# Feature transposes and their copy moved ahead of the numerators and of a weight piece's rounding, in the attention steps of an attention and two-layer kernel

## The chip, the cores and the metric

The kernel runs on one core of one Trainium2 chip. The metric is the device time of a whole execution in microseconds. Several executions are timed, and their median is the figure that counts. One more execution is recorded by the hardware profiler, and all rows below are from that one.

## The reference

Attention with random features, then two dense layers, all in float32:

```
phi(x) = exp(h - max(h)) / sqrt(m),  h = x @ omega.T - sum(x*x)/2
kv  = einsum('bhsm,bhsd->bhmd', phi(k), v);   z = sum_s phi(k)
num = einsum('bhsm,bhmd->bhsd', phi(q), kv);  den = phi(q) . z + 1e-6
x   = (num / den), heads side by side: 2304 tokens x 512
h = x @ w_in;  g = max(h,0) + alpha*min(h,0);  x = g @ w_out      (512 -> 2048 -> 512)
out = ((x @ w_a) * (x @ w_b)) @ w_out2                            (512 -> 1536 -> 512)
```

There are 4 batches, 8 heads, 576 positions, a head dimension of 64 and 128 features.

## The kernel before, in words

**Attention.** The 32 heads are handled as 8 units of four heads, and each unit as 5 tiles of up to 128 positions (the fifth has 64). One attention step `s` works on several tiles at once, as a software pipeline written out by hand. It projects the keys of tile `s` and the queries of another tile onto the features (`a_proj`, matmuls into the PSUM tiles `pp`), takes their negated maxima on VectorE (`a_max`, `nm`), and takes the exponentials on ScalarE (`a_exp`, `ph`). Then `attn_2` does four things. `a_kv` adds the key features of the step before into `kv`. `a_t` transposes on TensorE the query features that were made two steps before (PSUM tile `tp`) and copies them to SBUF (`phT`, line 798 where the copy is on ScalarE). `a_num` multiplies the transposed features that the step before left by `kv` into the PSUM tile `nd` and divides: three operations on VectorE, `rc`, its reciprocal, and `xn`. The fourth thing is the weight decoder, below. Last, `attn_3` calls `a_x`, which transposes the `xn` of the step before (PSUM tile `xp`) and copies it into the layer's input `xT` (line 839 where the copy is on ScalarE). The PSUM tiles `pp`, `tp`, `nd`, `xp` and the layer's `h` share five banks that go round. So the features are transposed two steps after their projection, their numerators follow one step later, and the transposes of the result one step after that.

**The decoder.** The weights come as 8-byte floats, and a weight piece of 128x512 is turned into two float32 halves, a rounded high one and a low one, whose products make up a precise matmul. `D_.go(n)` advances a Python generator `n` times, and each advance writes out a few instructions. For a piece in this stage (`piece`, line 283) the first three advances are the bits: four VectorE operations, on `z`, `a`, `c` and `c` again; in the first advance GpSimd is also given the scaling `z` of the next piece. The fourth advance is the rounding: `w<-a` on ScalarE (line 290), then a subtraction and an addition, `a<-a,w` and `w<-a,c` (lines 294 and 295), on GpSimd or on VectorE. In `attn_2` the call `D_.go(3)` writes out the bits ahead of everything else, and the call `D_.go()` behind the numerators writes out the rounding. Up to step 14 a piece is begun in about every second step, and from step 15 in each, until 17 pieces fill the places that there are.

**The order of the work.** Each engine takes its instructions in the order in which the program writes them. Until step 14 the attention steps stand alone. From step 15 a step is written inside a step of the first layer (`Mlp.step`): twelve matmuls of 256 columns (`h`), then the step's projections, key products, numerators and transposes, then twelve matmuls of the layer's second half (`y`), then `a_x`. The layer adds for each step `u` and `gh` on ScalarE and `h` and `gl` on VectorE.

**The planner's tallies.** Where an operation can go to two engines, `pick` (line 138) takes the way after which the largest of three tallies, `load["dve"]`, `load["act"]` and `load["pool"]`, is smallest; between equals it takes the first way. Every call books its estimated cost as it is written out, and `passed` takes an allowance of microseconds off all three at each step, 4.5 in steps 6 to 14. The feature copy books 0.62 on ScalarE or 0.70 on VectorE, the numerators of four slots book 0.87 on VectorE, and the copy of the transposed result books 0.41 on ScalarE or 0.37 on VectorE. Which engine gets a piece's subtraction and addition is settled in its first advance.

Of the kernel before, what the change touches and what calls it, by code (L numbers as in the profile page):

```python
# [65 lines left out]
def tile_kernel(ctx: ExitStack, tc: tile.TileContext, qT, kT, v1, omT, wbits, alpha, out):  # L66
# [71 lines left out]
    def pick(*ways):  # L138

        def worst(w):  # L140
            return max(load[e] + w.get(e, 0.0) for e in load)

        i = min(range(len(ways)), key=lambda i: worst(ways[i]))
        for e, x in ways[i].items():
            load[e] += x
        return i
# [579 lines left out]
    def slots_of(t):  # L726
        return 4 if t < 4 else 2

    def bank(name, pool=None):
        return (pool or psp[0]).tile([P, 512], F32, tag="ps", name=name)  # L730
# [39 lines left out]
    def a_kv(u, t):  # L770
        if t == 0:
            kvt[u] = pskv.tile([P, 4, D + 1], F32, tag="kv", name=f"kv{u}")
        kv = kvt[u]
        ph = phik.pop((u, t))
        for h in range(4):

            for r in (slice(0, M // 2), slice(M // 2, M)):
                tensor.matmul(kv[r, h, :], lhsT=ph[:, h if t < 4 else h % 2, r],
                                 rhs=t_v[u][:, t * VC + h * (D + 1):t * VC + (h + 1) * (D + 1)],
                                 start=(t == 0 and h == 0), stop=(t == 4 and h == 3))  # L780
        if t == 4:

            load["act"] += 0.4
            nc.scalar.activation(kvp[u % 3], kv, AF.Copy)
            kvt.pop(u)

    def a_t(u, t):

        ns = slots_of(t)
        ph = phiq.pop((u, t))  # L790
        pp = bank(f"tp{u}_{t}").rearrange("p (o m) -> p o m", m=P)
        for h in range(ns):
            tensor.transpose(pp[:, h, :], ph[:, h, :], ident)
        d = pq.tile([P, 4, P], F32, tag="phT", name=f"phT{u}_{t}", bufs=2)
        if pick({"act": 0.1 + 0.13 * ns}, {"dve": 0.1 + 0.15 * ns}):
            vector.tensor_copy(d[:, :ns], pp[:, :ns])
        else:
            nc.scalar.activation(d[:, :ns], pp[:, :ns], AF.Copy)
        phT[u, t] = d

    def a_num(u, t):


        ns = slots_of(t)
        d = phT.pop((u, t))
        kv = kvp[u % 3]
        nd = bank(f"nd{u}_{t}")[:, :4 * (D + 1)].rearrange("p (o e) -> p o e", e=D + 1)
        for h in range(ns):
            for a in range(2):
                r = slice(a * 64, a * 64 + 64)  # L810

                tensor.matmul(nd[r, h, :], lhsT=d[:, h, r], rhs=kv[:, h if t < 4 else 2 * a + h, :],
                                 start=True, stop=True)
        load["dve"] += 0.35 + 0.13 * ns
        rc = sm.tile([P, 4], F32, tag="rc", name=f"rc{u}_{t}")
        vector.tensor_scalar(out=rc[:, :ns], in0=nd[:, :ns, D], scalar1=EPS * M, scalar2=None, op0=ALU.add)
        vector.reciprocal(out=rc[:, :ns], in_=rc[:, :ns])
        xn = pq.tile([P, 4, D], F32, tag="xn", name=f"xn{u}_{t}", bufs=2)
        vector.tensor_tensor(out=xn[:, :ns], in0=nd[:, :ns, 0:D],
                                in1=rc[:, :ns].unsqueeze(2).to_broadcast([P, ns, D]), op=ALU.mult)  # L820
        xns[u, t] = xn
# [20 lines left out]
    ev = {n: {} for n in ("k", "kv", "q", "t", "num", "x")}  # L842
# [6 lines left out]
    for b in range(NB):  # L849
        u = HG * b  # L850
        for i, ut in enumerate([(u, 0), (u, 1), (u + 1, 0), (u + 1, 1), (u, 2), (u, 3), (u, 4),
                                (u + 1, 2), (u + 1, 3), (u + 1, 4)]):
            s = HG * TT * b + Q_LAG + i
# [37 lines left out]
    def attn_2(s):  # L891

        D_.go(3)
        if s in late:
            held[late[s]] = ev["kv"][s]
        elif s in ev["kv"]:
            for ut in (held.pop(s, None), ev["kv"][s]):
                if ut:
                    a_kv(*ut)
        if s in ev["num"]:  # L900
            a_num(*ev["num"][s])
        D_.go()
        if s in ev["t"]:
            a_t(*ev["t"][s])

    def attn_3(s):
        if s in ev["x"]:
# [20 lines left out]
    if True:  # L928
        w_ = bank("warm")
        for i in range(WARM):  # L930
            tensor.matmul(w_[:, 0:P], lhsT=warm, rhs=warm, start=True, stop=True)
        for s in range(SPLIT_AT):
            D_.step(DEC0[0] if s < 3 else DEC0[1] if s < Q_LAG else DEC0[2])
            passed(1.3 if s < Q_LAG else 4.5)
            pj = attn_1(s)
            nm = a_max(*pj)
            loads(s)

            for k in range(KT):
                if s > x_step[k // 2, (CI - 1) // P]:  # L940
                    A.split(0, 0, CI, k)
            a_exp(*pj, nm)
            if s == 3:
                D_.start(0)
            if s == Q_LAG + 1:
                nc.sync.dma_start(out=bend, in_=alpha)
            attn_2(s)
            attn_3(s)
        vector.tensor_scalar(out=bend, in0=bend, scalar1=-1.0, scalar2=1.0, op0=ALU.mult, op1=ALU.add)
    st_z.close()  # L950

    with st_m:
# [4 lines left out]
        def attn_next(high=None, low=None):  # L957
            s = nxt_s[0]
            nxt_s[0] += 1
            D_.step(DEC1)  # L960
            pj = attn_1(s)
            if high:
                high()
            if pj:
                nm = a_max(*pj)
            loads(s)
            if low:
                low()
            if pj:
                a_exp(*pj, nm)  # L970
            attn_2(s)
            A.after.append(lambda: attn_3(s))
# [381 lines left out]
```

## Time and profile before

| what | us |
|---|---|
| median of the runs (3) | 956.07 |
| lowest and highest | 954.65, 956.70 |
| the profiled execution, its own time | 954.51 |
| span of the profiled execution | 952.7 |
| busy: TensorE, VectorE, ScalarE, GpSimd | 937.4, 677.1, 483.3, 130.6 |

The span runs from the first to the last instruction of the profiled execution; its own time is 1.8 us longer. Matmuls are pipelined and their ends are modelled, so a busy TensorE isn't one at its peak. In the rows PE is TensorE, PEld its weight loads, DVE VectorE, ACT ScalarE, POOL GpSimd. A row of the order in time has the start, the duration, the engine and line, the operation, the written tile and what it reads, and in brackets the idle time before it with what ended it. Most TensorE and VectorE instructions go through a helper and show its line, L188, so tiles tell them apart. The granted TensorE clock is at full speed (1.00) in every stretch.

### The profile page before, as it was taken

To read this page: it belongs to the slowest core of one execution; us is meant where nothing else is said; L and a number is where in the kernel's file an instruction comes from. 1 tells how busy PE (TensorE), PEld (TensorE's weight loads), DVE (VectorE), ACT (ScalarE), POOL (GpSimd) and SP (SyncE) were. 2 spreads that over 40 slices of the span, in tenths; PEclk is the share of its full clock that TensorE was granted. 3 is DMA by queue.
4 is the path that set the end of the run, shared out by engine and by line. 5 is a ranking of instruction groups with operands and counts; after the bars stand their busy time and mean duration, and the time that the engine had idled before them with its cause. 6 is when DMAs were issued, how large, how long until landed. Compare 5 with 4: busy or idle time off the path is not lost.

```text
span 952.7 us, 16709 instructions
## 1 busy us (share of the span) xinstructions
PE 937.4 (98%) x6486; PEld 845.7 (89%) x6486; DVE 677.1 (71%) x1359; ACT 483.3 (51%) x1149; POOL 130.6 (14%) x110
## 2 busy tenths in 40 slices
PE   8889999999999999999999999999999999999998
PEld 7778999999988888889888899999999998989896
DVE  5898854554488888788787977888397867473633
ACT  5876766654344445244444455564364654454541
POOL 3686700000001111010010000000011111110201
PEclk9999999999999999999999999999999999999999
DMA  8544422000133232325538656259829379624323
GB/s 301 172 164 146 140 77 77 26 23 24 46 88 111 89 130 92 133 70 196 184 126 298 254 210 221 78 177 360 305 85 264 94 215 331 181 34 100 47 53 67
DMA packets 49279, 137.88 MB, mean 145 GB/s; under 512 B 4528, under 2 KB 11056, under 8 KB 49200
## 3 DMA queue, kind: packets, MB, share of 16 engines
q1 hardware_dynamic: 44304, 128.03, 38.6%
q0 software_dynamic: 4752, 8.65, 6.0%
q8 instruction: 51, 0.84, 0.4%
q14 instruction: 28, 0.23, 0.1%
q10 hardware_dynamic: 144, 0.13, 0.0%
HBM read 90.14 MB, written 46.66 MB: 144 GB/s over the span
## 4 chain that ended last, share of the span: by engine, by line
PE 91%; DVE 5%; ACT 3%; issue 1%; ACTq 0%; DVEq 0%
PE y L188 21%; PE h L188 20%; PE W L188 16%; PE o L188 15%; PE E L188 8%; PE B L188 4%; ACT ph L765 2%; PE tp L188 1%; PE nd L188 1%; PE kv L188 1%; PE xp L188 1%; DVE c L188 1%; DVE a L188 0%; DVE xl L505 0%; DVE h L188 0%
## 5 line engine op out<-in xcount | busy, mean ns | idle before, releaser
L188 PE MATMUL h<-xh,w 128*128 128x256 f32 (+1 forms) x768 | 204.4, 340 | 0.2 <-DVE yo L188 0.2
L188 PE MATMUL y<-gh,w 128*128 128x256 f32 (+1 forms) x768 | 201.9, 338 | 0.3 <-ACT gh L545 0.3
L188 PEld LDWEIGHTS h<-xh,w 128*128 128x128 f32 x768 | 135.0, 189 | 15.7 <-DVE yo L188 0.4
L188 PEld LDWEIGHTS y<-gh,w 128*128 128x128 f32 x768 | 134.5, 189 | 15.5 <-ACT gh L545 0.5
L188 PE MATMUL o<-w,gh 128*128 128x512 f32 x432 | 133.2, 390 | 0.0
L188 PE MATMUL h<-xl,w 128*128 128x512 f32 (+1 forms) x384 | 129.1, 336 | 0.3 <-DVE xl L505 0.3
L188 PE MATMUL y<-gl,w 128*128 128x512 f32 (+1 forms) x384 | 129.1, 336 | 0.1
L188 DVE SCALAR_TENSOR_TENSOR h<-u,bend,h 128x256 f32<-128x256 f32 (+1 forms) x96 | 59.4, 619 | 58.9 <-ACT u L533 58.5
L533 ACT ACTIVATE u<-h 128x256 f32<-128x256 f32 (+1 forms) x96 | 47.1, 491 | 103.9 <-PE h L188 100.6
L188 PEld LDWEIGHTS o<-w,gh 128*128 128x128 f32 x432 | 81.0, 188 | 16.4
L545 ACT ACTIVATE gh<-h 128x256 fp32r<-128x256 f32 (+1 forms) x96 | 47.1, 491 | 86.0 <-DVE h L188 85.9
L188 PE MATMUL o<-w,gl 128*128 128x512 f32 x216 | 84.2, 390 | 0.0
L1253 POOL DMA_DIRECT2D out<-op x30 | 26.3, 875 | 418.1 <-ACT op L163 337.3
L188 PEld LDWEIGHTS h<-xl,w 128*128 128x128 f32 x384 | 72.7, 189 | 7.9 <-DVE xl L505 0.5
L188 PEld LDWEIGHTS y<-gl,w 128*128 128x128 f32 x384 | 72.8, 190 | 7.8 <-DVE gl L188 0.3
L505 POOL TENSOR_TENSOR xl<-xT,xh 128x512 fp32r<-128x512 f32 (+1 forms) x19 | 25.5, 1358 | 342.8 <-ACT xh L501 187.1
L188 DVE TENSOR_TENSOR gl<-h,gh 128x256 fp32r<-128x256 f32 (+1 forms) x96 | 53.1, 554 | 22.0 <-ACT gh L545 21.4
L163 ACT ACTIVATE u<-W 128x384 f32<-128x384 f32 x72 | 35.1, 492 | 45.7 <-PE W L188 44.4
L163 ACT ACTIVATE op<-o 128x512 f32<-128x512 f32 x51 | 30.4, 597 | 50.7 <-PE o L188 44.8
L188 DVE SCALAR_TENSOR_TENSOR a<-raw,z 128x512 uint32<-128x512 uint32 x68 | 51.1, 751 | 2.1
L188 DVE SCALAR_TENSOR_TENSOR c<-raw,c 128x512 f32<-128x512 uint32 x68 | 48.5, 713 | 2.3
L188 PEld LDWEIGHTS o<-w,gl 128*128 128x128 f32 x216 | 40.6, 188 | 8.4
(491 smaller groups left out, 1942.2 us busy)
## 6 DMA issues: line engine op xcount, KB each, us to landing
raw<-in_w SPq DMA_DIRECT2D x68, 512.0 KB, 4.2
w<-store SPq DMA_DIRECT2D x44, 512.0 KB, 6.9
store<-t_None SPq DMA_DIRECT2D x39, 512.0 KB, 3.0
st<-ypart SPq DMA_DIRECT2D x14, 768.0 KB, 7.0
out<-op POOLq DMA_DIRECT2D x30, 256.0 KB, 5.3
q<-in_qT SPq DMA_DIRECT2D x8, 576.0 KB, 3.8
v<-in_v SPq DMA_DIRECT2D x7, 650.0 KB, 5.8
yp<-ypart SPq DMA_DIRECT2D x4, 1024.0 KB, 7.8
```

What stands on the lines that cost most here:

```text
L163: nc.scalar.activation(out, in_, AF.Copy)
L188: return call(*a, **k)
L505: (nc.vector, nc.gpsimd)[way].tensor_tensor(out=lo, in0=src, in1=hi.bitcast(F32), op=ALU.subtract)
L533: nc.scalar.activation(u_, hp, AF.Relu, scale=-1.0)
L545: nc.scalar.activation(gh, hp, AF.Copy)
L765: nc.scalar.activation(ph[:, 2 * pr + j], pair[j][:, o + pr], AF.Exp, bias=nm[:, j, o + pr:o + pr + 1])
L1253: nc.gpsimd.dma_start(out=dst, in_=op, accum_op=ALU.add)
```

## The change

In `attn_2` the call of `a_t` moves from the end to a place ahead of `a_num`. The order was bits, key products, numerators, rounding, transposes with their copy; it becomes bits, key products, transposes with their copy, numerators, rounding.

```diff
@@ -897,11 +897,11 @@
             for ut in (held.pop(s, None), ev["kv"][s]):
                 if ut:
                     a_kv(*ut)
+        if s in ev["t"]:
+            a_t(*ev["t"][s])
         if s in ev["num"]:
             a_num(*ev["num"][s])
         D_.go()
-        if s in ev["t"]:
-            a_t(*ev["t"][s])
 
     def attn_3(s):
         if s in ev["x"]:
```

## Rows read from the trace of the kernel before

The kinds of row are those of the section on time and profile.

**Rows 1.** Busy time by stage: stretch, length, then busy us of each engine

```profile
14.00:45.00 31.00, 26.12 (x432) 21.91 (x429) 27.64 (x63) 26.08 (x88) 19.61 (x14) 1.00 0.70 238
...
45.00:125.00 80.00, 75.99 (x942) 68.45 (x940) 69.60 (x160) 53.88 (x167) 55.91 (x38) 1.00 0.42 137
...
125.00:240.00 115.00, 114.33 (x1371) 106.95 (x1372) 59.52 (x179) 68.31 (x216) 0.00 (x0) 1.00 0.14 45
```

**Rows 2.** Groups by line and shape, 0 to 330 us: copies and rounding

```profile
L798 ACT ACTIVATE phT<-tp 128x512 f32<-128x512 f32 x32 | 20.0, 624 | 0.0
...
L839 ACT ACTIVATE xT<-xp 128x256 f32<-128x256 f32 x26 | 10.3, 398 | 5.2 <-PE xp L188 5.1
...
L188 DVE COPY xT<-xp 128x256 f32<-128x256 f32 x6 | 2.5, 419 | 2.2 <-PE xp L188 2.2
...
L290 ACT ACTIVATE w<-a 128x512 fp32r<-128x512 f32 x28 | 18.1, 645 | 11.7 <-DVE a L188 11.5
```

**Rows 3.** Who waited for whom, TensorE alone, 14 to 125 us

```profile
PE nd L188 <- ACT phT L798: 2.5, 4, 1.2
...
PE pp(4, 1)_False L188 <- ACT phT L798: 0.2, 1, 0.2
```

**Rows 4.** ScalarE in order of time, step 8

```profile
22.29 2.22 ACT L765 ACTIVATE ph<-pp(1, 3)_False,nm(0, 1, 3)_443 128x128 f32<-128x128 f32 x8
...
24.29 0.75 ACT L290 ACTIVATE w<-a 128x512 fp32r<-128x512 f32 x1
...
24.81 0.71 ACT L798 ACTIVATE phT<-tp 128x512 f32<-128x512 f32 x1
```

**Rows 5.** TensorE in order of time, steps 9 and 10

```profile
23.71 0.69 PE L188 MATMUL kv<-v,ph 128*64 128x65 f32 x16
...
25.57 0.69 PE L188 MATMUL nd<-kvp,phT 128*64 128x65 f32 x16 [1.18 <-ACT phT L798]
...
26.19 0.66 PE L188 MATMUL tp<-ident,ph 128*128 128x128 f32 x4
...
26.78 0.71 PE L188 MATMUL pp(2, 0)_False<-xT,k 64*128 64x128 f32 x8
```

**Rows 6.** VectorE in order of time: idle times, 28 to 48 us

```profile
28.04 1.29 DVE L188 TENSOR_REDUCE nm(0, 2, 0)_544<-pp(2, 0)_False 128x4 f32<-128x512 f32 x2 [0.90 <-PE pp(2, 0)_False L188]
...
34.79 1.02 DVE L188 TENSOR_REDUCE nm(0, 2, 2)_671<-pp(2, 2)_False 128x3 f32<-128x384 f32 x2 [0.20 <-PE pp(2, 2)_False L188]
...
43.33 0.76 DVE L505 TENSOR_TENSOR xl<-xT,xh 128x256 fp32r<-128x256 f32 x2 [0.30 <-ACT xh L501]
```

**Rows 7.** Groups by line and shape, 0 to 330 us: VectorE, two widths

```profile
L188 DVE SCALAR_TENSOR_TENSOR h<-u,bend,h 128x256 f32<-128x256 f32 x40 | 19.4, 486 | 34.7 <-ACT u L533 34.5
...
L188 DVE SCALAR_TENSOR_TENSOR h<-u,bend,h 128x512 f32<-128x512 f32 x15 | 11.3, 752 | 5.0 <-ACT u L533 4.9
```

**Rows 8.** Who waited for whom, 14 to 125 us: around the rounding

```profile
POOL a L294 <- ACT w L290: 25.2, 15, 6.0
...
ACT w L290 <- DVE a L188: 1.8, 6, 0.5
```

**Rows 9.** GpSimd, then TensorE, in order of time: piece 6, its reader

```profile
58.41 1.28 POOL L295 TENSOR_TENSOR w<-a,c 128x512 fp32r<-128x512 f32 x1
...
61.30 0.36 PE L188 MATMUL h<-xh,w 128*128 128x256 f32 x1
```

**Rows 10.** VectorE twice, then GpSimd, in order of time: one decode operation

```profile
76.22 0.42 DVE L188 TENSOR_SCALAR z<-z 128x512 uint32<-128x512 uint32 x1
...
81.17 0.76 DVE L188 TENSOR_SCALAR z<-z 128x512 uint32<-128x512 uint32 x1
...
81.00 1.53 POOL L251 TENSOR_SCALAR z<-raw 128x512 f32<-128x512 f32 x1
```

**Rows 11.** TensorE, then VectorE, in order of time: numerators and reader

```profile
80.17 0.64 PE L188 MATMUL nd<-kvp,phT 128*64 128x65 f32 x16
...
83.77 0.15 DVE L188 TENSOR_SCALAR rc<-nd 128x4 f32<-128x4 f32 x1
```

## The prediction

> **What bounds the kernel now.** I read the busy time by stage first. The moved call runs only in the attention steps, which end before 240 us. From 125 to 240 us TensorE is busy 114.33 of 115 us, with VectorE at 59.52 and ScalarE at 68.31 [rows 1]: there TensorE is the bound, and an order inside the step can't give it more than the 0.67 us that it idles. From 14 to 45 us the picture is another one: VectorE is busy 27.64 of 31 us, ScalarE 26.08, TensorE 26.12, and from 45 to 125 us TensorE idles 4.0 us of 80, with VectorE at 69.60 [rows 1]. So only the stretch from 14 to 125 us is open, and what counts in it is VectorE's line of work and what holds TensorE.
>
> The second view is TensorE's waits in that stretch. The numerators wait four times for the feature copy, 2.5 us together, and once a projection waits 0.2 us for it [rows 3]. The third view shows why. At step 8 ScalarE finishes its exponentials, rounds a piece at 24.29 and only then copies the features at 24.81 [rows 4]; TensorE has ended the key products at 24.40 and starts the numerators at 25.57, after 1.18 us idle [rows 5]. The rounding, whose result GpSimd needs and nobody else soon, stands ahead of a copy that TensorE needs in the next step.
>
> The fourth view is VectorE in order of time, since a wait of TensorE is only worth what it passes on. From 28 to 48 us VectorE idles three times: 0.90 us for a projection, 0.20 us for another and 0.30 us for the rounding of the layer's input on ScalarE, 1.40 us together [rows 6]. The rest of that stretch it works without a gap.
>
> **The change part by part.** Nothing is removed or added in the program's text: four transposes and one copy go ahead of 16 matmuls and three VectorE operations, and ahead of the rounding (one ScalarE operation and, for the 17 pieces of this stage, two on GpSimd). The moved call issues no DMA, nor do the numerators and the rounding, so SP's queue is as it was, and GpSimd's queue keeps its own order.
>
> *TensorE.* The transposes' inputs were made two steps earlier, so they can run as soon as the key products end. At step 9 the transposes would fill 0.6 us from 24.40 on [rows 5]. At step 8 the copy would start at 24.29 instead of 24.81, 0.52 us earlier, and with its 0.71 us end at 25.00 [rows 4]. The numerators then start at about 25.0 and end 0.6 us later, at 25.6; the next projection, which before followed the transposes at 26.78 [rows 5], starts at 25.6, over a microsecond earlier. The first idle time of VectorE, 0.90 us, goes. The same swap takes out the other three waits on the copy, and with them most of the 0.20 us.
>
> *Which engine copies.* This is the part that the diff doesn't show. All 40 feature copies are on ScalarE now (the row has the 32 wide ones), and a few result copies are on VectorE [rows 2]. `a_t` now picks before `a_num` has booked its 0.87 on VectorE. Take a step of the first stage in which no piece is begun, such as 11 or 13. The maxima book 8 x 0.17 = 1.36 on VectorE and the exponentials 8 x 0.28 = 2.24 on ScalarE. Before, the copy saw VectorE at 1.36 + 0.87 = 2.23: on ScalarE the largest tally becomes 2.86, on VectorE 2.93, so ScalarE. After, it sees 1.36: on VectorE that is 2.06, below ScalarE's 2.24, so the copy goes to VectorE. The result copy then sees VectorE at 2.93 and ScalarE at 2.24 and goes to ScalarE (largest tally 2.93 against 3.30); before, it saw 2.23 and 2.86 and went to VectorE (2.86 against 3.27). Step 9 flips its feature copy too (1.02 + 0.70 = 1.72 against 1.68 + 0.62 = 2.30) and has no result copy. In steps with a piece VectorE carries 2.3 more and nothing flips. From step 15 on VectorE's tally runs ahead as long as there is a piece in each step, and what flips long after that lies where TensorE is the bound.
>
> So VectorE gets three wide feature copies and loses two result copies of 0.42 us [rows 2]. The trace has no copy of 512 columns from PSUM on VectorE. It can't cost less than the 256-column copy, 0.42 [rows 2], nor should it cost more than a two-input operation of 512 columns, 0.75 [rows 7]. I take 0.68: the 0.42 plus what the two-input operation adds from 256 to 512 columns, 0.752 - 0.486 = 0.266 [rows 7]. Then VectorE's line grows by 3 x 0.68 - 2 x 0.42 = 1.20 us (by the bounds, 0.42 to 1.41).
>
> *The rest of ScalarE.* The rounding now comes behind the copy, about 0.5 us later (the copy's place in rows 4 is 0.5 to 0.7 us). Where ScalarE waited for the decoder's bits before the rounding, 1.8 us in six cases [rows 8], the copy fills the gap and the delay is smaller. The sum of ScalarE's work ahead of the result copy is the same, so the result copy and the layer's input rounding stand where they stood, or come up to 0.5 us earlier. That, with the result copy's move, covers the 0.30 us of the last idle time.
>
> *Who waits for the later rounding.* GpSimd's subtraction does; it waits for it 25.2 us in 15 cases [rows 8], so GpSimd shifts. What waits for GpSimd is the layer's matmul that reads the low half. The nearest case is piece 6: its addition ends at 59.69, and its reader starts at 61.30 [rows 9]. A delay of 0.5 us, and a reader that comes a little earlier, fit in those 1.6 us, so I cost it at nothing; were that cover gone, TensorE would idle for what is beyond it.
>
> *Who waits for the later numerators.* They come one set of transposes, 0.6 us, later on TensorE. Their first reader on VectorE stands behind the bits: in a typical step the numerators start at 80.17 and end by 80.8, and the reader comes at 83.77 [rows 11]. Behind that reader VectorE has the next step's `h` and maxima. With 3 us of cover it costs nothing in steps with a piece. In steps without one the copy, or the maxima, stand in front of it.
>
> **The sum.** VectorE's line loses 1.40 us of idle time and gains 1.20 us of copies: 0.2 us less (by the bounds of the copy, 1.0 less to nothing). From 45 us on the work of a step is the same on each engine and the 0.2 us is handed through. The 0.2 us of the one projection [rows 3] falls in a stretch in which VectorE has no gap, and I count nothing for it. Against the profiled execution's own time that is 954.51 - 0.2 = 954.3 us. The median of the runs stands 1.56 us above that execution, so the forecast is 956.07 - 0.2 = 955.9 us. A measurement of this kernel can tell about 0.2%, 1.9 us, from no change: this is no measurable change.
>
> **The rivals.**
>
> *TensorE's waits come back in full.* If the numerators' 2.5 us and the projection's 0.2 us [rows 3] were the true bound, the time would be 956.07 - 2.7 = 953.4 us. For it: each ends at the copy, and the copy stood behind the rounding. Against it: VectorE has only 1.40 us of idle time to give where these waits lie [rows 6]. Chance 0.13.
>
> *The swap costs and nothing comes back.* The change then does something else than it says: it moves work onto the fullest engine. If the three idle times only shift to another wait (the next one in line is VectorE's maxima behind the copy), the line grows by the 1.20 us: 957.3 us. Chance 0.12.
>
> *Nothing passes.* Gains and copies end inside the waits that TensorE has anyway between 45 and 125 us, 4.0 us in all [rows 1]: 956.1 us. Chance 0.18.
>
> *VectorE meets GpSimd (slower).* The `z` operation of a piece takes 0.42 us alone and took 0.76 us when it began right behind the start of a GpSimd operation of 1.53 us [rows 10]; 7 of the 17 in this stage took 0.6 us or more. A rounding 0.5 us later shifts GpSimd's three operations against VectorE's bits. If the ten undisturbed ones were all caught, VectorE would lose 10 x 0.34 = 3.4 us, and the time would be 955.9 + 3.4 = 959.3 us. It passes the 1.9 us from the seventh on. Against it: seven already are caught, and a shift frees some as it catches others. The Trainium skill, "SBUF — State Buffer", section "SBUF: two separate sides", says that VectorE and GpSimd share a pair of SBUF ports under an exclusive lock, so that the later of the two stops until the other's instruction ends. By that rule the loss in rows 10 would have been the 1.36 us to the end of GpSimd's operation and not 0.34; the trace bears out a collision, but not one of full length. With 1.36 us each, ten more would make 13.6 us and a time of 969.5 us, and two would already decide. Chance 0.06.
>
> **How the numbers follow.** The forecast has the remaining 0.51. Faster by over 0.2% is the first rival alone, 0.13; slower is the last, 0.06; the forecast and the two middle rivals (957.3 and 956.1 us are both within 1.9 us) make 0.81 for no change. The range takes in the forecast with the copy's bounds, 955.1 to 956.1 us, and the swap at 957.3, and leaves out the two outer rivals, 0.19. The runs of before lie from 954.65 to 956.70, so I add 1.2 us below and 0.6 us above: 953.9 to 957.9 us.
>
> **What would show it.** Right: three feature copies on VectorE ahead of 45 us at 0.65 to 0.7 us each, two result copies fewer there; TensorE's wait of the numerators for the copy near zero; the idle 0.90 us of VectorE at 28 us down to about 0.2; the stage from 125 us on begun 0 to 0.5 us earlier. Wrong: numerators that still wait for the copy, a projection or a maximum that waits for a copy on VectorE, layer matmuls that wait for GpSimd's addition, `z` operations of 0.7 us or more in over ten of the 17, or a second stage whose busy time has changed.

## The result, and the profile after

| what | before | after |
|---|---|---|
| median of 5 runs each, us | 955.58 | 960.39 |
| lowest and highest, us | 954.65, 956.70 | 959.66, 962.03 |
| profiled execution, its own time and span, us | 954.51, 952.7 | 960.39, 958.6 |

The ratio is 1.0059, 95% interval [1.0046, 1.0073]: the kernel became slower by 4.8 us, and the whole interval lies above the 0.2% that a measurement can tell. The forecast was no change, 955.9 us in a range up to 957.9.

What the change was to do early, it did. First ScalarE in order of time at step 8, as in [rows 4] (start, duration, engine, line, operation):

```profile
24.16 0.72 ACT L798 ACTIVATE phT<-tp 128x512 f32<-128x512 f32 x1
24.64 0.76 ACT L290 ACTIVATE w<-a 128x512 fp32r<-128x512 f32 x1
```

And TensorE at steps 9 and 10, as in [rows 5]:

```profile
24.20 0.66 PE L188 MATMUL tp<-ident,ph 128*128 128x128 f32 x4
24.93 0.69 PE L188 MATMUL nd<-kvp,phT 128*64 128x65 f32 x16
25.55 0.71 PE L188 MATMUL pp(2, 0)_False<-xT,k 64*128 64x128 f32 x8
```

The copy now precedes the rounding, the numerators start at 24.93 instead of 25.57 with no idle time of 1.18 us ahead of them, and the next projection comes at 25.55 instead of 26.78. TensorE's waits from 14 to 135 us (engine, tile, line, whom it waited for, total us, times, longest) have no row of the numerators for the copy any more:

```profile
PE xp L188 <- ACT ph L765: 2.4, 3, 1.6
PE kv L188 <- ACT ph L765: 2.0, 3, 0.8
...
PE nd L188 <- DVE xn L188: 0.3, 1, 0.3
```

The copies by line and shape, 0 to 330 us, as in [rows 2]:

```profile
L798 ACT ACTIVATE phT<-tp 128x512 f32<-128x512 f32 x27 | 17.3, 641 | 0.0
L839 ACT ACTIVATE xT<-xp 128x256 f32<-128x256 f32 x32 | 13.1, 409 | 10.7 <-PE xp L188 10.6
L188 DVE COPY phT<-tp 128x512 f32<-128x512 f32 x5 | 3.4, 681 | 0.0
```

Five wide feature copies went to VectorE, at 681 ns each, and all result copies to ScalarE. VectorE got 3.4 us of wide feature copies and lost the 2.5 us of result copies of [rows 2], which is too little for 4.8 us. The busy time by stage, as in [rows 1], does not say at first sight where they lie:

```profile
14.00:45.00 31.00, 27.91 (x438) 22.91 (x436) 29.06 (x65) 25.85 (x89) 19.55 (x14) 1.00 0.69 237
45.00:125.00 80.00, 75.48 (x932) 67.17 (x933) 70.21 (x157) 52.62 (x164) 55.00 (x38) 1.00 0.41 135
125.00:240.00 115.00, 114.63 (x1342) 103.86 (x1338) 58.97 (x173) 67.63 (x214) 0.00 (x0) 1.00 0.14 46
```

From 125 to 240 us TensorE is as busy as before, 114.63 us against 114.33, and has done 1342 matmuls where it had done 1371. It idles no more than before and gets less done. To see when, I follow one landmark through both traces: the first matmul `h` of each first-layer group. The 13th and the 36th, before:

```profile
119.16 0.36 PE L188 MATMUL h<-xh,w 128*128 128x256 f32 x1
...
236.90 0.36 PE L188 MATMUL h<-xh,w 128*128 128x256 f32 x1
```

And after:

```profile
119.45 0.36 PE L188 MATMUL h<-xh,w 128*128 128x256 f32 x1
...
241.50 0.36 PE L188 MATMUL h<-xh,w 128*128 128x256 f32 x1
```

| group | 1st | 9th | 13th | 24th | 32nd | 36th |
|---|---|---|---|---|---|---|
| start before, us | 44.07 | 95.14 | 119.16 | 181.31 | 222.06 | 236.90 |
| after less before, us | -1.15 | -0.01 | +0.29 | +2.86 | +4.53 | +4.60 |

The first layer matmul starts 1.15 us earlier, the gain is used up by the ninth group, and from the 13th to the 36th the changed kernel takes 122.05 us where the other took 117.74: 4.31 us more, with hardly any idle time on TensorE. The busy time of that stretch (stretch, length, then TensorE, its weight loads, VectorE, ScalarE, GpSimd, the granted clock, DMA share and GB/s), before and after:

```profile
119.16:236.90 117.74, 116.89 (x1422) 108.96 (x1421) 62.58 (x186) 69.06 (x218) 2.31 (x2) 1.00 0.14 46
119.45:241.50 122.05, 121.68 (x1422) 110.42 (x1421) 63.45 (x183) 69.91 (x220) 2.14 (x2) 1.00 0.14 44
```

The same 1422 matmuls keep TensorE busy for 121.68 us instead of 116.89, at the same clock, and it idles 0.37 us instead of 0.85. Another 1.3 us come between 566 and 572 us of the kernel before, long behind the attention; they are left open below. Together, -1.15 + 1.44 (up to the 13th group) + 4.31 + 1.3 make the 5.9 us that lie between the two profiled executions; the medians lie 4.8 us apart.

One step there, number 1 of unit 7, TensorE in order of time. Before:

```profile
172.64 0.69 PE L188 MATMUL kv<-v,ph 128*64 128x65 f32 x16
173.16 0.64 PE L188 MATMUL nd<-kvp,phT 128*64 128x65 f32 x16
173.73 0.66 PE L188 MATMUL tp<-ident,ph 128*128 128x128 f32 x4
174.14 0.36 PE L188 MATMUL y<-gh,w 128*128 128x256 f32 x1
```

After:

```profile
174.84 0.69 PE L188 MATMUL kv<-v,ph 128*64 128x65 f32 x16
175.45 0.66 PE L188 MATMUL tp<-ident,ph 128*128 128x128 f32 x4
176.04 0.69 PE L188 MATMUL nd<-kvp,phT 128*64 128x65 f32 x16
176.66 0.38 PE L188 MATMUL y<-gh,w 128*128 128x256 f32 x1
```

The same records of matmuls, 16, 16 and 4, take 1.50 us from the first key product to `y` before and 1.82 us after: 0.32 us more for another order. Look at the part of the array that a row names (rows times columns, 128*64 or 128*128). Key products and numerators fill half its columns, transposes and layer matmuls all. The old order changes the shape once behind the key products, the new one three times. From 130 to 232 us, the median time from the start of the last matmul of one kind to the start of the first of the next:

| boundary | before, ns | after, ns |
|---|---|---|
| `kv` to `nd`, same shape | 49 (12 times) | none |
| `nd` to `tp`, change | 150 (19) | none |
| `tp` to `y`, same shape | 28 (14) | none |
| `kv` to `tp`, change | none | 150 (12) |
| `tp` to `nd`, change | none | 202 (18) |
| `nd` to `y`, change | none | 149 (14) |

Since they run from start to start, these times contain the pace of the earlier kind; inside the groups before, the mean is 31 ns between key products, 29 between numerators and 131 between transposes. In a step that has all three boundaries they sum to 0.501 us against 0.227, 0.27 us more; the other 0.05 us of the step are the numerators themselves, 0.62 us to the next start where it was 0.57 with a boundary of the same length behind them. Why they take longer behind transposes is not shown. In that window: 12 x 0.101 + 18 x 0.052 + 14 x 0.121 = 3.84 us. Between the two landmarks, with the boundaries of every kind counted, the boundaries add 3.8 us and the matmuls inside the groups 1.0 us (0.7 of it the numerators), and TensorE idles 0.5 us less: 4.3 us.

### The profile page after: what moved, and what is told of

Its sections match the earlier page's. It is cut to its first block, busy times and chain, and to the rows that moved or that the text cites. A ratio compares the mean times of both kernels' runs of the same rounds, so it can differ in the third digit from the quotient of the medians.

```text
span 958.6 us, 16703 instructions
## 1 busy us (share of the span) xinstructions
PE 944.2 (98%) x6486; PEld 846.7 (88%) x6486; DVE 680.8 (71%) x1358; ACT 483.2 (50%) x1150; POOL 129.7 (14%) x110
## 4 chain that ended last, share of the span: by engine, by line
PE 86%; DVE 9%; ACT 2%; DMA 2%; issue 1%; SPq 0%; ACTq 0%; DVEq 0%
PE h L188 20%; PE y L188 19%; PE o L188 15%; PE W L188 14%; PE E L188 7%; PE B L188 3%; PE nd L188 1%; DVE c L188 1%; DMA store<-t_None 1%; PE tp L188 1%; ACT ph L765 1%; PE kv L188 1%; DVE a L188 1%; PE xp L188 1%; DVE h L188 1%
```

## The experiments

Theory A: TensorE is held up wherever consecutive matmuls change the shape of the array, and the change adds two such places to each step. Theory B: the feature copies that moved to VectorE cost the time. Theory C: the later rounding does, through GpSimd and its collisions with VectorE. Each kernel was timed 5 to 12 times, beside the kernel before on the same chip, whose median stands in brackets. "Step" below is the time from the first key product to `y` in step 1 of unit 7 (in the first experiment from the first transpose, which there stands in front; the eighth has no such stretch), "loss" the lag behind the kernel before that is added between the 13th and the 36th group; both are from one profile of each kernel.

| experiment | order in the step | median, us (before) | ratio, interval | step, us | loss, us |
|---|---|---|---|---|---|
| (before) | kv, nd, rounding, tp | | 1 | 1.50 | 0 |
| (after) | kv, tp, nd, rounding | 960.39 (955.58) | 1.0059 [1.0046, 1.0073] | 1.82 | 4.31 |
| e1_transposes_first | tp, kv, nd, rounding | 957.87 (955.05) | 1.0032 [1.0020, 1.0044] | 1.67 | 2.82 |
| e2_numerators_first | kv, nd, tp, rounding | 953.68 (955.05) | 0.9993 [0.9984, 1.0003] | 1.50 | 0.02 |
| e3_half_transposes | as after, tp in halves | 962.31 (955.05) | 1.0084 [1.0070, 1.0097] | 1.96 | 7.24 |
| e4_copies_scalar | as after | 960.50 (955.05) | 1.0061 [1.0049, 1.0074] | 1.82 | 4.29 |
| e5_rounding_early | kv, rounding, tp, nd | 961.75 (954.22) | 1.0073 [1.0061, 1.0085] | 1.81 | 4.28 |
| e6_split_transposes | kv, half nd, half tp, half nd, half tp, with the rounding behind nd | 961.19 (954.22) | 1.0067 [1.0054, 1.0080] | 1.80 | 5.04 |
| e7_wide_numerators | as after, nd on all columns | 962.98 (954.22) | 1.0080 [1.0068, 1.0093] | 1.92 | 5.51 |
| e8_transposes_at_layer | tp ahead of the projections | 955.95 (954.44) | 1.0017 [1.0008, 1.0026] | | 1.50 |
| e9_numerators_first_again | kv, nd, tp, rounding | 953.55 (954.44) | 0.9991 [0.9982, 1.0001] | 1.49 | 0.02 |

**One change of shape more instead of two.** In `attn_2`, against the kernel after, the transposes go ahead of the key products:

```diff
         D_.go(3)
+        if s in ev["t"]:
+            a_t(*ev["t"][s])
         if s in late:
...
-        if s in ev["t"]:
-            a_t(*ev["t"][s])
         if s in ev["num"]:
```

> Theory A (array shape): a change between matmuls that fill half of the array's columns (key products, numerators) and those that fill all of them (transposes, layers) holds TensorE up by 0.15 to 0.2 us, and the changed kernel has two such changes more in each step. With the transposes ahead of the key products there is one more than in the kernel before, so from 130 to 230 us a step should lose about 0.17 us against before, half of the changed kernel's 0.33: 957.5 us (956.5 to 958.5). Theory B (the copies that went to VectorE) and theory C (the later rounding and GpSimd's collisions) have the same copies and the same rounding as the changed kernel: 960.4 us (959.5 to 961.5), with the same 0.33 us a step.

Measured 957.87 us. TensorE in order of time, the same step:

```profile
172.86 0.66 PE L188 MATMUL tp<-ident,ph 128*128 128x128 f32 x4
...
174.53 0.39 PE L188 MATMUL y<-gh,w 128*128 128x256 f32 x1
```

The step is 0.17 us longer than before, about half of the 0.32, and the loss 2.82 us, between nothing and 4.31. That is A's half-way house. That the total lies so near A's figure is partly luck: in the profile the first layer matmul comes 1.66 us earlier than before, and 1.65 us are lost behind 560 us, neither of which A forecast.

**The numerators first, the rounding still last.** This undoes the part of the change that touches TensorE's order and keeps the part that moves the copy ahead of the rounding:

```diff
         if s in ev["num"]:
             a_num(*ev["num"][s])
-        D_.go()
         if s in ev["t"]:
             a_t(*ev["t"][s])
+        D_.go()
```

(against the kernel before.)

> Key products, numerators, transposes, and the rounding last: the numerators are back in front, the rounding stays behind the copy. A: the same number of shape changes as before, so no loss from 130 us on, and the gain of the earlier copy stays: 954.7 us (953.7 to 955.7). B: the copies pick behind the numerators' booking again, so all are on ScalarE: 955.6 us, as before. C: the rounding is as late as in the changed kernel: 960.4 us (959.5 to 961.5).

Measured 953.68 us, at the lower end of A's range. TensorE in order of time, the same step:

```profile
170.67 0.69 PE L188 MATMUL kv<-v,ph 128*64 128x65 f32 x16
...
172.17 0.36 PE L188 MATMUL y<-gh,w 128*128 128x256 f32 x1
```

The step is back at 1.50 us and the loss is 0.02 us over 23 groups. With the old order on TensorE the loss goes; the later rounding, which this kernel keeps, costs nothing, so C falls here. B is not told apart, since this kernel also has its feature copies back on ScalarE.

**The same shape by force.** Against the kernel after, each transpose is written as two matmuls by the identity on half the columns, so that key products, transposes and numerators have one shape:

```diff
         for h in range(ns):
-            tensor.transpose(pp[:, h, :], ph[:, h, :], ident)
+            for r in (slice(0, P // 2), slice(P // 2, P)):
+                tensor.matmul(pp[r, h, :], lhsT=ph[:, h, r], rhs=ident, start=True, stop=True)
```

> The changed kernel with each transpose as two matmuls with the identity that fill half of the columns each, so that key products, transposes and numerators have one shape. A: no change of shape between them; TensorE's loss of 0.33 us a step goes and the gain of about 1 us at the first layer matmul stays: 954.7 us (953.7 to 956). B and C: copies and rounding are untouched: 960.4 us (959.5 to 961.5).

Measured 962.31 us, outside A's range: a miss. TensorE in order of time, the same step of this kernel:

```profile
176.44 0.69 PE L188 MATMUL kv<-v,ph 128*64 128x65 f32 x16
176.96 1.04 PE L188 MATMUL tp<-ident,ph 128*64 128x128 f32 x16
177.83 0.64 PE L188 MATMUL nd<-kvp,phT 128*64 128x65 f32 x16
178.40 0.38 PE L188 MATMUL y<-gh,w 128*128 128x256 f32 x1
```

From key products to transposes it is now 0.52 us (0.61 after): that boundary fell to 50 ns, as A has it, and from transposes to numerators it fell to 103 ns from 202. But the transposes themselves leave 16 records instead of 4 and last 0.87 us to the next start instead of 0.59. The edit costs more than it removes, so it speaks for the price of these two boundaries and not for the total.

**All feature copies on ScalarE.** Against the kernel after:

```diff
-        if pick({"act": 0.1 + 0.13 * ns}, {"dve": 0.1 + 0.15 * ns}):
-            vector.tensor_copy(d[:, :ns], pp[:, :ns])
-        else:
-            nc.scalar.activation(d[:, :ns], pp[:, :ns], AF.Copy)
+        load["act"] += 0.1 + 0.13 * ns
+        nc.scalar.activation(d[:, :ns], pp[:, :ns], AF.Copy)
```

> The changed kernel with all 40 feature copies on ScalarE. A: nothing about the shapes changes: 960.4 us (959.4 to 961.4), 0.33 us a step as in the changed kernel. B: the loss goes: 955.6 us (954.6 to 956.6). C: 960.4 us.

Measured 960.50 us with a loss of 4.29 us. Where the copies run does not matter; B falls.

**The rounding back ahead of the copy.** Against the kernel after, `D_.go()` moves up behind the key products:

```diff
+        D_.go()
         if s in ev["t"]:
             a_t(*ev["t"][s])
         if s in ev["num"]:
             a_num(*ev["num"][s])
-        D_.go()
```

> The changed kernel with the rounding back ahead of the copy: key products, rounding, transposes, numerators. TensorE's order is the changed kernel's. A: the same 0.33 us lost in a step from 130 us on, and the early gain of about 1 us mostly gone as well, since the copy stands behind the rounding again: 961.3 us (960 to 962.5). B: 960.4 us. C: the rounding is as early as in the kernel before: 955.6 us (954.6 to 956.6).

Measured 961.75 us with a loss of 4.28 us: the rounding's place has nothing to do with it, and C falls a second time. The half of A's text that concerns the start fell too: the first layer matmul was 1.61 us earlier than before, so the early gain doesn't need the later rounding.

**The kernel before, with only changes of shape added.** Against the kernel before, half of the transposes is written between the two halves of the numerators; the copy, the rounding and all other orders stay:

```diff
         for h in range(ns):
+            if mid and h == ns // 2:
+                a_t_half(*mid)
             for a in range(2):
...
         if s in ev["num"]:
-            a_num(*ev["num"][s])
+            a_num(*ev["num"][s], ev["t"].get(s))
```

`a_t_half` is the first `ns // 2` transposes of `a_t`, which later writes the others and the copy.

> The kernel before, with the first half of a step's transposes written between the two halves of its numerators: rounding, copies and their engines as before, and two more changes of shape in each step, as many as the changed kernel has more. A: 0.3 us lost in a step from 130 us on, as in the changed kernel, and no early gain: 960.5 us (959 to 962). B and C: nothing of theirs is touched: 955.3 us (954.3 to 956.3).

Measured 961.19 us. TensorE in order of time, the same step of this kernel:

```profile
176.12 0.69 PE L188 MATMUL kv<-v,ph 128*64 128x65 f32 x16
176.64 0.40 PE L188 MATMUL nd<-kvp,phT 128*64 128x65 f32 x8
176.97 0.44 PE L188 MATMUL tp<-ident,ph 128*128 128x128 f32 x2
177.34 0.45 PE L188 MATMUL nd<-kvp,phT 128*64 128x65 f32 x8
177.73 0.44 PE L188 MATMUL tp<-ident,ph 128*128 128x128 f32 x2
177.92 0.36 PE L188 MATMUL y<-gh,w 128*128 128x256 f32 x1
```

1.80 us to `y`, 0.30 more than before, with two changes of shape more and the same matmuls on TensorE. The PSUM banks, which go round in the order in which the tiles are asked for, keep that order too. From `nd` to `tp` it takes 150 ns (38 times) and from `tp` to `nd` 203 (19 times) between 130 and 232 us. This is the experiment that shows A most plainly: the loss comes without the change itself.

**Numerators on all columns.** Against the kernel after, for the tiles with four slots one matmul of 128 columns takes the place of two of 64:

```diff
                 r = slice(a * 64, a * 64 + 64)
+                if t < 4:
+                    r = slice(0, P)
+                    if a:
+                        continue
```

> The changed kernel with the numerators of the full tiles as one matmul over all columns in place of two over half of them each (the fifth tiles stay halved), so that transposes, numerators and layer matmuls have one shape. A: in four of five steps the two changes behind the transposes go, one stays in front of them; if the wide numerators take no longer than the two halves side by side, the loss from 130 us on shrinks to under a third and the early gain stays: 955 us (954 to 957). Should the gaps between the groups go and the numerators take longer by as much, that shows in the rows. B and C: 960.4 us (959.5 to 961.5).

Measured 962.98 us, outside A's range of 954 to 957 us. TensorE in order of time, the same step:

```profile
178.11 0.69 PE L188 MATMUL kv<-v,ph 128*64 128x65 f32 x16
178.73 0.66 PE L188 MATMUL tp<-ident,ph 128*128 128x128 f32 x4
179.22 1.00 PE L188 MATMUL nd<-kvp,phT 128*128 128x65 f32 x8
180.03 0.36 PE L188 MATMUL y<-gh,w 128*128 128x256 f32 x1
```

The boundaries behind the transposes shrink as A has it (`tp` to `nd` 109 ns instead of 202, `nd` to `y` 83 instead of 149). The numerators then last 0.81 us to the next start instead of 0.62, which is the confound that the expectation names: the total tells nothing between the theories.

**The transposes where the array is full already.** Against the kernel after, `a_t` moves from `attn_2` to the top of `attn_1`, behind the layer's `h` matmuls and ahead of the projections:

```diff
     def attn_1(s):
+        if s in ev["t"]:
+            a_t(*ev["t"][s])
...
-        if s in ev["t"]:
-            a_t(*ev["t"][s])
         if s in ev["num"]:
```

> Transposes and their copy still further in front: ahead of the step's projections, right behind the layer's matmuls, which fill all columns too; then projections, key products, numerators, rounding. The copy still comes ahead of numerators and rounding, as in the changed kernel. A: as many changes of shape as in the kernel before, so no loss in a step from 130 us on, and what the earlier copy gives stays: 954 us (952.5 to 955.5). B (copies pick ahead of the numerators' booking) and C (rounding behind the numerators): 960.4 us (959.5 to 961.5).

Measured 955.95 us, ratio 1.0017 [1.0008, 1.0026], 0.45 us above A's range and far below that of B and C: a loss of 1.50 us stays, which A did not forecast. Part of it is at the boundaries: from `h` over `tp` to the projections 0.122 + 0.202, and from `nd` to `y` 0.149, against 0.209 from `h` to the projections, 0.150 and 0.028 before, so 0.473 against 0.387, 0.09 us more in a step. The number of changes is the same; what is lost is the cheap way from the transposes to `y`. So the count of changes alone does not give the time. In this kernel the layer's matmuls also wait where before the transposes `xp` did, and in the third row for longer than the 0.3 us of before (TensorE's waits, 14 to 240 us):

```profile
PE h L188 <- ACT ph L765: 2.4, 4, 1.3
PE h L188 <- DVE gl L188: 2.4, 6, 0.9
PE h L188 <- DVE xl L505: 1.2, 2, 0.8
```

The busy time between the 13th and the 36th group shares out the 1.50 us:

```profile
119.85:239.09 119.24, 117.78 (x1422) 109.15 (x1421) 63.81 (x187) 70.41 (x219) 2.69 (x2) 1.00 0.14 45
```

TensorE idles 1.46 us where it idled 0.85, so 0.6 us are waits; the other 0.9 us are 117.78 us of busy time instead of 116.89 for the same 1422 matmuls.

**The numerators first, once more.** The kernel of the second experiment again, to see whether its small gain is one.

> The kernel of the second experiment once more (numerators, transposes, rounding last), to narrow its interval: 0.999 to 1.000 of the kernel before if its gain of 0.07% is real, with an interval that stays below 1; 1.000 or above if it was chance. No loss in a step from 130 us on in either case.

Measured 953.55 us against 954.44, ratio 0.9991 [0.9982, 1.0001], with a loss of 0.02 us in its profile as in the first case. Twice the same 0.07 to 0.09% below the kernel before, but the interval does not stay below 1, as was asked of a real gain: no version is shown to beat the kernel before.

## Why the prediction was wrong

**The step that failed** is in the sum: "From 45 us on the work of a step is the same on each engine". With it stands the sentence that bounds TensorE, "an order inside the step can't give it more than the 0.67 us that it idles", which looks only at what an order could give and never at what it could take. The order of TensorE's matmuls was costed at nothing, as if their time were the sum of their lengths. This is the term that was put at nothing: it measured 0.32 us a step in the step shown and 4.3 us between the 13th and the 36th group. The rows to price it stood in the trace of before: 49 and 28 ns where the shape stays, 150 where it changes, and the shapes are written in every row (128*64, 128*128 in [rows 5]). A view of starts from one matmul to the next would have given 150 + 150 + 150 less 227 ns, some 0.22 us a step, for the order `kv`, `tp`, `nd`, `y`.

The Trainium skill, "TensorEngine Tiling (Array Packing)", section "Key Properties", says that changing the tiling mode, and not just the tile, makes TensorE drain. The trace agrees with a hold-up there: 150 to 202 ns from start to start at a change between 128*64 and 128*128, 28 and 49 ns at the two boundaries without one. The page gives no price, and by its sentence alone the change adds two drains to each step.

**TensorE's wait for the copy: right.** Predicted were numerators at about 25.0 and the next projection at 25.6; they came at 24.93 and 25.55. The wait of 2.5 us [rows 3] is gone. But the rounding ahead of the copy was only part of its cause. In the second experiment, with the rounding behind the copy and the transposes behind the numerators, the numerators still wait 2.0 us for it in three cases (0.67 us where it was 1.18 at step 9). What takes the rest away is the transposes in front of the numerators, which fill that time on TensorE (24.20 to 24.86 above). The fifth experiment fits: its rounding is ahead of the copy and its transposes in front, and the numerators don't wait, though its granted clock is lower there and TensorE waits 1.1 us for the copy at other tiles.

**Which engine copies: right, by the tallies.** Three wide feature copies on VectorE before 45 us, as worked out (25.58, 32.93 and 40.25), at 0.68 us each, the value that was taken between 0.42 and 0.75; the two result copies went the other way. In all, 6 of the 40 feature copies flipped.

**VectorE's line: right in sign, too small.** Its three idle times [rows 6] are gone. The layer's first `h` operation on VectorE came at 47.00 instead of 47.62, 0.62 us earlier where 0.2 was predicted, and the layer's first matmul 1.15 us earlier. "The 0.2 us is handed through" was wrong in the other direction than one would fear: more was gained and none of it arrived, because it was used up by the ninth group, at 95 us, and 1.44 us were lost up to the 13th.

**The later rounding and numerators: right that the rounding costs nothing.** The second and the fifth experiment have the rounding behind and ahead of the copy, and TensorE's order decides the loss in both. The later numerators had less cover than was thought: from 125 us on their first reader `rc` on VectorE waits for them, 1.9 us in seven cases, where it never did before. VectorE is busy for 58.97 of 115 us there, so it is not the bound.

**The rivals.** *VectorE meets GpSimd* forecast 959.3 us, the nearest figure, and had the wrong cause: 4 of the 17 `z` operations took 0.6 us or more and a fifth 0.597, fewer than the seven before. *The swap costs and nothing comes back* fell: the three idle times did go, and in the fourth experiment the loss is the same with no copy on VectorE. *Nothing passes* was right that the early gain was gone by the ninth group, and had nothing of the loss behind it. *TensorE's waits come back in full* fell too: the waits went and the time is 960.4 us. With the old order of TensorE and the copy ahead of the rounding the time is 953.6 us, but both intervals reach 1 and most of the wait is still there. What was named as a sign that the prediction is wrong, "a second stage whose busy time has changed", came only in part: the busy time hardly moved, 114.63 us instead of 114.33, but 1342 matmuls were done in it instead of 1371.

**What stays open.** First, the 1.3 us at 566 to 572 us, where the instructions have the same order in both kernels. In the wait view there, 560 to 600 us, the changed kernel has a row that the one before hasn't:

```profile
PE o L188 <- ACT w L163: 0.6, 1, 0.6
```

It appears in the first, fourth and fifth experiment as well (0.4 to 0.6 us) and in no other. What brings it on was not tried by itself. Second, where the early gain comes from. The fifth experiment has it without the later rounding. The second has it, 1.46 us, though the first idle time of [rows 6] is still there. Before, after, first and second have a granted clock of 1.00 in every stretch up to 45 us, so in these the clock does not explain it; the fifth has 0.81 and 0.76 from 18 to 26 us and is early all the same. Each is a single profile, and in others the clock moves the start more than that, which the last section is about.

## What to carry to other kernels

Where TensorE is the bound, the order of its matmuls has a price of its own: group those that fill the same part of the array, and count the changes of shape in a step before and after an edit. Here each one more made the step 0.15 to 0.17 us longer (0.17 for one, 0.30 and 0.32 for two); which neighbours remain matters too, as the eighth experiment shows. Here neither busy shares nor waits showed it; the time from the start of one matmul to the start of the next did, and so did a landmark followed through both traces. A wait that was taken away early in the pipeline was worth nothing, because a later stage, bound elsewhere, paid more for the new order in each step.

## What was not expected of the hardware

The granted clock of TensorE in the early stretch is not the same in each execution of one kernel. The second and the ninth experiment are the same kernel. Busy time by stretch (length, then TensorE, its weight loads, VectorE, ScalarE, GpSimd, the granted clock, DMA share and GB/s), the second:

```profile
18.00:22.00 4.00, 2.63 (x36) 1.88 (x34) 3.97 (x7) 2.79 (x12) 3.92 (x4) 1.00 1.02 407
22.00:26.00 4.00, 3.33 (x60) 2.84 (x62) 3.53 (x10) 4.00 (x16) 2.04 (x2) 1.00 0.68 216
```

And the ninth:

```profile
18.00:22.00 4.00, 1.07 (x18) 0.74 (x17) 3.93 (x8) 2.51 (x9) 3.04 (x4) 0.88 0.84 298
22.00:26.00 4.00, 4.00 (x44) 3.32 (x42) 3.23 (x8) 3.41 (x13) 2.10 (x2) 0.50 0.31 104
26.00:30.00 4.00, 4.00 (x72) 3.50 (x68) 1.91 (x7) 2.22 (x7) 3.51 (x3) 0.77 0.62 235
```

From 18 to 22 us TensorE was busy 1.07 of 4 us in the ninth and 2.63 in the second. In the ninth the granted clock then fell to 0.50, the lower of its two levels (1.2 GHz), from 22 to 26 us, with TensorE busy throughout, and rose again after that; in the second it stayed at 1.00. The idle time of that one stretch is not the whole story: TensorE was busy 1.90 us of it in the first experiment and 2.25 in the third, and the clock from 22 to 26 us was 1.00 and 0.62. The first layer matmul came 1.46 us earlier than before in the second and 1.19 us later in the ninth, 2.65 us apart for one and the same program. So a difference of a microsecond or two at 45 us, in a single profile, can't be laid to an edit unless the clock in front of it is the same; the loss between the 13th and the 36th group, 0.02 us in both, is free of that.
